# Unit maxima by way of memory in place of a product of ones

## The chip, the cores and the metric

The kernel runs on one core of a Trainium2 chip. The metric is device time in microseconds (us) of one execution. A core has TensorE (PE, matmuls; PEld are its weight loads), VectorE (DVE), ScalarE (ACT), GpSimd (POOL) and SyncE (SP), which here only issues transfers. Each engine works through its own queue in order. Times are given as a median of several executions; one further execution is taken with the hardware profiler, and its trace gives all rows that are shown here.

## The reference: what is computed

There are 8 batches of 8 heads, 576 positions and 64 channels per head. An attention without a score matrix comes first, then two layers that mix over positions and over channels:

```python
q_s = softmax(q, axis=-1)                    # over the 64 channels
k_s = softmax(k, axis=2)                     # over the 576 positions
kv  = einsum('bhsd,bhse->bhde', k_s, v)
x   = einsum('bhsd,bhde->bhse', q_s, kv)     # heads side by side: x is (8, 576, 512)
xt  = x.transpose(0, 2, 1)
u   = x + (relu(xt @ w_tok1) @ w_tok2).transpose(0, 2, 1)     # 576 -> 256 -> 576
out = u + relu(u @ w_ch1) @ w_ch2                             # 512 -> 1536 -> 512
```

Both softmaxes subtract the maximum first. The one that matters here is k's: one maximum for each of the channels, taken over all positions.

## The kernel before

The attention and the first mixing layer work on *units*: two heads of one batch, 128 channels side by side. There are 8 x 4 = 32 units, numbered from 0; NJ is 4, the units of a batch. The second mixing layer works on 9 groups of 512 rows of u; for each group it runs 12 *steps* (f). A step is `ch1` (line 409: 12 matmuls of 128 x 512 into a bank of the PSUM ring `ps_h`), an eviction by ACT (line 412, `h2h`) and by DVE (line 413, `h2l`, the rest that the first rounding leaves), and `ch2` (line 421: 12 matmuls into the four `ps_o` banks). The `ch2` of a step stands behind the `ch1` of the next.

A unit goes through these stages: its loads (`load_unit`: `kt` with the channels on partitions, line 137; `q`, line 140; `k` with the positions on partitions, line 144), `softmax_k` and `softmax_q`, then `stage_qT` (transposes q), `stage_kv` (line 277: 20 records of small matmuls, k's exponentials against v with a column of ones for the sums), `stage_y` (line 337), `stage_h1` (line 345) and two halves of `stage_u` (line 381). The first NE = 8 units are done ahead of the steps ("early"); the other 24 are dealt out between the steps by the table `todo`: at its own step a unit n runs `stage_qT` and `stage_kv`, then `softmax` of unit n + 1, then, half a step later, the loads of unit n + 2.

In a late unit `k` lies with positions on partitions, while the maximum is found from `kt` by DVE as one value for each of 128 partitions (`mc`, line 219). To subtract it, the maximum of every channel must stand in every partition. That is done in lines 233 to 236: ACT writes a diagonal matrix `dg` with the maxima, PE multiplies a matrix of ones by it into a bank of `ps_h`, and ACT copies the result to `mb`. POOL then subtracts `mb` from `k` (line 237) and ACT takes the exponential (line 238). `mb` and `dg` have one buffer each, `mc` two, `k` and `q` two, `kt` and `v` one.

What sets the order: the kernel's text gives a priority by its order, and the builder lays out each engine's queue with a model of durations, so that an engine may run ahead of the text where its buffers allow. All loads are on SP's queue (`v`, lines 154 and 155, is issued in `stage_kv`, for the next unit). The results go out on ACT's queue (line 454). `split` (lines 114 and 115) makes a rounded copy on ACT and the rest on DVE or, for `qh` and `ql`, on POOL.

Of the kernel before, what the change touches and what calls it, by code (L numbers as in the profile page):

```python
# [8 lines left out]
F32 = mybir.dt.float32  # L9
F32R = mybir.dt.float32r  # L10
U32 = mybir.dt.uint32
AF = mybir.ActivationFunctionType
# [3 lines left out]
P = 128  # L16
# [4 lines left out]
def attn_mixer_kernel(ctx: ExitStack, tc: tile.TileContext, q, k, kt, v, wt, out, dims):  # L21
# [3 lines left out]
    nc = tc.nc  # L25
    B, H, S, D, TOK, DM, DCH, wide = dims
    NJ = DM // P
# [8 lines left out]
    NE = 2 * NJ  # L36
# [13 lines left out]
    ident = const.tile([P, P], F32R, name="ident")  # L50
# [11 lines left out]
    ones = const.tile([P, P], F32, name="ones")  # L62
# [26 lines left out]
    dg = lay.tile([P, P], F32, name="dg")  # L89
    for i in range(3):  # L90
        slots[i][1] = lay.tile([P, NJ, CW], F32R, name=f"ul{i}")
    mb = lay.tile([P, P], F32, name="mb")
# [16 lines left out]
    def f32(ap):  # L109
        return ap.bitcast(F32)  # L110
# [8 lines left out]
    def ps_unit(dtype=F32):  # L119

        pools = unit_banks[0]
        pool, name = pools[turn[0] % len(pools)]
        turn[0] += 1
        return pool.tile([P, 512], dtype, name=name)
# [88 lines left out]

    turned_k = []

    def softmax_k(u):
        ktt = u["kt"]
        mc = sm.tile([P, 1], F32, name="mc")
        nc.vector.tensor_reduce(mc, ktt, axis=AX.X, op=ALU.max)  # L219
        kx = u["k"]  # L220
        if u["early"]:
            nc.vector.tensor_scalar(mc, mc, -1.0, None, op0=ALU.mult)
            nc.scalar.activation(ktt, ktt, AF.Exp, bias=mc)
            t = ps_unit()
            for c in range(C):
                nc.tensor.transpose(t[:, c * P : (c + 1) * P], ktt[:, c * P : (c + 1) * P], f32(ident))
            nc.scalar.copy(kx[:, 0:C, :], t.rearrange("p (c d) -> p c d", c=C))
            t = ps_unit()
            turned_k.append(nc.tensor.transpose(t[:, 0:P], ktt[:, S0 : S0 + P], f32(ident)).ins)
            nc.scalar.copy(kx[:, C, :], t[:, 0:P])  # L230
            return

        nc.scalar.activation(dg, f32(ident), AF.Copy, scale=mc)
        t = ps_unit()
        nc.tensor.matmul(t[:, 0:P], ones, dg, start=True, stop=True)  # L235
        nc.scalar.copy(mb, t[:, 0:P])  # L236
        nc.gpsimd.tensor_tensor(kx, kx, mb.unsqueeze(1).broadcast_to([P, C1, P]), op=ALU.subtract)  # L237
        nc.scalar.activation(kx, kx, AF.Exp)

# [223 lines left out]
    def soft(n):  # L463
        if n < NU:
            softmax_k(units[n])
            softmax_q(units[n])
# [194 lines left out]
```

## Time and profile before

| | us |
|---|---|
| median of 3 executions (lowest to highest) | 822.23 (821.69 to 822.65) |
| the profiled execution | 822.09 |
| its span, first to last instruction | 820.3 |
| PE busy | 803.5 (98%) |
| PE weight loads busy | 678.1 (83%) |
| DVE busy | 490.5 (60%) |
| ACT busy | 340.0 (41%) |
| POOL busy | 84.4 (10%) |

The time of the profiled execution and its span differ by 1.8 us, which lie outside the first and the last instruction. A row of a group gives line, engine, operation, the tiles written and read with their shapes, the count, then busy time in us and the mean duration in ns, and last the idle time of the engine just before these instructions with what ended it. A row of the order of time gives start, duration, engine, line and operation; neighbours of one kind are merged ("x20"), with in brackets an idle time before them. A row of the chain of waits gives start and length of a piece of the chain that ended last. SPq is SP's queue: an issue of a transfer. Matmuls overlap each other in the trace; a matmul's start is recorded, its end is modelled.

### The profile page before, as it was taken

The numbers are of one execution on the slowest core, as the hardware profiler recorded it, in microseconds if no ns is written. First come the engines' busy times: TensorE is split into PE (matmuls) and PEld (weight loads), VectorE is DVE, ScalarE is ACT, GpSimd is POOL, SyncE is SP. The second block draws the span as 40 slices with busy tenths as digits, with TensorE's granted clock in tenths as the row PEclk, the third lists the DMA queues.
The fourth block names the chain that finished last, engine by engine and source line by source line (L and its number), as shares of the span: only waits on it lengthen the run. The fifth ranks groups of instructions, "written<-read, shape, count | busy, mean of one in ns | idle before, by whom it ended". The sixth has DMA issues, their size and how long they took to land.

```text
span 820.3 us, 11946 instructions
## 1 busy us (share of the span) xinstructions
PE 803.5 (98%) x4512; PEld 678.1 (83%) x4512; DVE 490.5 (60%) x1104; ACT 340.0 (41%) x898; POOL 84.4 (10%) x69
## 2 busy tenths in 40 slices
PE   7899999989999999999999999999999999999997
PEld 6688888878888888888888888888888888888886
DVE  6999998897875455855576555845575324113112
ACT  6976564457544344443434443434443421101110
POOL 1000010102201011111111111101111100000100
PEclk9999999999999999999999999999999999999999
DMA  9753433424222112312232221312121001001001
GB/s 298 241 161 93 150 108 113 139 83 126 64 73 85 48 53 63 109 52 64 64 114 63 64 64 35 113 47 63 39 91 48 15 1 51 1 1 51 1 1 51
DMA packets 60634, 63.55 MB, mean 77 GB/s; under 512 B 40865, under 2 KB 40993, under 8 KB 60577
## 3 DMA queue, kind: packets, MB, share of 16 engines
q1 hardware_dynamic: 55392, 53.36, 22.2%
q10 hardware_dynamic: 5184, 9.44, 3.1%
q8 instruction: 35, 0.57, 0.3%
q14 instruction: 23, 0.18, 0.1%
HBM read 53.35 MB, written 9.44 MB: 77 GB/s over the span
## 4 chain that ended last, share of the span: by engine, by line
PE 89%; DVE 6%; DMA 3%; ACT 1%; SPq 1%; issue 0%; DVEq 0%; ACTq 0%
PE ps_h L409 34%; PE ps_o L421 34%; PE ps_h L381 8%; PE ps_h L337 5%; PE ps_h L277 2%; DMA stg<-in_w 2%; PE ps_h L345 1%; DMA kt_t<-in_kt 1%; PE ps_o L381 1%; PE ps_h L235 1%; PE ps_o L337 1%; DVE mc L219 1%; DVE q_t L323 1%; DVE cv_s L176 1%; DVE cv_s L181 1%; DVE stg L179 0%
## 5 line engine op out<-in xcount | busy, mean ns | idle before, releaser
L409 PE MATMUL ps_h<-uh,cw 128*128 128x512 f32 x864 | 268.6, 391 | 0.3 <-DVE cw L115 0.3
L421 PE MATMUL ps_o<-h2h,cw 128*128 128x512 f32 x864 | 250.0, 392 | 2.2 <-DVE cw L115 2.2
L421 PEld LDWEIGHTS ps_o<-h2h,cw 128*128 128x128 f32 x864 | 160.0, 188 | 34.7 <-ACT h2h L412 2.4
L409 PEld LDWEIGHTS ps_h<-uh,cw 128*128 128x128 f32 x864 | 159.3, 188 | 31.6 <-DVE cw L115 0.8
L413 DVE SCALAR_TENSOR_TENSOR h2l<-ps_h,h2h 128x512 fp32r<-128x512 f32 x108 | 74.3, 688 | 170.4 <-ACT h2h L412 170.2
L412 ACT ACTIVATE h2h<-ps_h 128x512 fp32r<-128x512 f32 x108 | 64.4, 596 | 253.8 <-PE ps_h L409 251.5
L409 PE MATMUL ps_h<-ul,cw 128*128 128x512 f32 x432 | 168.7, 390 | 0.0
L421 PE MATMUL ps_o<-h2l,cw 128*128 128x512 f32 x432 | 151.9, 394 | 0.0
L409 PEld LDWEIGHTS ps_h<-ul,cw 128*128 128x128 f32 x432 | 81.1, 188 | 17.4
L421 PEld LDWEIGHTS ps_o<-h2l,cw 128*128 128x128 f32 x432 | 79.7, 188 | 15.9
L323 DVE COPY q_t<-cv_s 32x160 f32<-32x160 f32 (+1 forms) x264 | 62.1, 235 | 45.2 <-POOL ql L115 41.9
L237 POOL TENSOR_TENSOR k_t<-k_t,mb 128x640 f32<-128x640 f32 x24 | 38.0, 1583 | 350.6 <-ACT mb L236 350.6
L115 POOL TENSOR_TENSOR ql<-q_t,qh 128x640 fp32r<-128x640 f32 x24 | 39.2, 1633 | 220.7 <-ACT qh L114 218.2
L245 DVE TENSOR_REDUCE st<-q_t 128x10 f32<-128x640 f32 x32 | 26.2, 817 | 38.2 <-DMA q_t<-in_q 38.2
L323 ACT COPY q_t<-cv_s 32x128 f32<-32x128 f32 (+1 forms) x120 | 36.8, 307 | 2.1 <-DVE cv_s L315 0.7
L256 ACT ACTIVATE q_t<-q_t 128x640 f32<-128x640 f32 x24 | 17.7, 739 | 40.4 <-DVE q_t L255 40.4
L381 PE MATMUL ps_h<-w2h,hh 128*128 128x256 f32 (+1 forms) x112 | 32.6, 299 | 0.0
L381 PE MATMUL ps_h<-w2l,hh 128*128 128x256 f32 (+1 forms) x112 | 32.6, 296 | 0.0
L389 DVE TENSOR_TENSOR ul<-ps_h,uh 128x320 fp32r<-128x320 f32 (+4 forms) x76 | 26.8, 372 | 7.4 <-ACT uh L388 6.8
L388 ACT CAST uh<-ps_h 128x320 fp32r<-128x320 f32 (+4 forms) x76 | 24.4, 337 | 15.6 <-PE ps_h L381 11.2
L381 PE MATMUL ps_h<-w2h,hl 128*128 128x320 f32 (+1 forms) x112 | 29.8, 300 | 0.3 <-DVE hl L353 0.2
L219 DVE TENSOR_REDUCE mc<-kt_t 128x1 f32<-128x640 f32 x32 | 25.9, 809 | 4.8 <-DMA kt_t<-in_kt 3.5
(144 smaller groups left out, 1077.8 us busy)
## 6 DMA issues: line engine op xcount, KB each, us to landing
stg<-in_w SPq DMA_DIRECT2D x28, 512.0 KB, 4.0
kt_t<-in_kt SPq DMA_DIRECT2D x32, 320.0 KB, 3.2
q_t<-in_q SPq DMA_DIRECT2D x32, 320.0 KB, 3.1
v_t<-in_v SPq DMA_DIRECT2D x64, 128.0 KB, 2.6
out<-stg ACTq DMA_DIRECT2D x32, 256.0 KB, 2.1
k_t<-in_k SPq DMA_DIRECT2D x24, 320.0 KB, 3.3
v_t<-in_v SPq DMA_DIRECT2D x32, 32.0 KB, 2.5
out<-part ACTq DMA_DIRECT2D x4, 256.0 KB, 2.3
```

The source lines that it names most:

```text
L115: lo_eng.tensor_tensor(lo, src, f32(hi), op=ALU.subtract)
L219: nc.vector.tensor_reduce(mc, ktt, axis=AX.X, op=ALU.max)
L237: nc.gpsimd.tensor_tensor(kx, kx, mb.unsqueeze(1).broadcast_to([P, C1, P]), op=ALU.subtract)
L245: nc.vector.tensor_reduce(st[:, 0, :], qt, axis=AX.X, op=ALU.max)
L323: eng(qx[ys, 0:n, xs], turned[xs, 0:n, ys])
L337: nc.tensor.matmul(y[:, 0:TOK], a, w, start=(i == 0), stop=(i == len(mm) - 1))
L381: nc.tensor.matmul(t[:, 0:N], a, w, start=(i == 0), stop=(i == len(mm) - 1))
L389: nc.vector.tensor_tensor(ul, src, f32(uh), op=ALU.subtract).ins,
L409: nc.tensor.matmul(t, cw[f][x][:, n, :], w, start=(i == 0), stop=(i == 3 * NJ - 1))
L412: nc.scalar.activation(hh, t, AF.Relu).ins,
L413: nc.vector.scalar_tensor_tensor(hl, t, 0.0, f32(hh), op0=ALU.max, op1=ALU.subtract).ins,
L421: nc.tensor.matmul(o, cw[f][x][:, n, :], w, start=(first and i == 0), stop=(last and i == 2))
```

## The change

From unit NE + NJ = 12 on, the maximum takes another way to all partitions: `mc` is written to a row of 128 values in memory, and that row is read back into `mb`, the same row for each of the 128 partitions. Both transfers are on SP's queue; the second reads what the first has written. The row has two buffers. `dg`, the product of ones and the copy to `mb` remain for units 8 to 11; units 0 to 7 never had them.

```diff
+    THROUGH = NE + NJ
+    dram = ctx.enter_context(tc.tile_pool(name="dram", bufs=2, space=bass.MemoryType.DRAM))
...
-        nc.scalar.activation(dg, f32(ident), AF.Copy, scale=mc)
-        t = ps_unit()
-        nc.tensor.matmul(t[:, 0:P], ones, dg, start=True, stop=True)
-        nc.scalar.copy(mb, t[:, 0:P])
+        if u["n"] < THROUGH:
+            nc.scalar.activation(dg, f32(ident), AF.Copy, scale=mc)
+            t = ps_unit()
+            nc.tensor.matmul(t[:, 0:P], ones, dg, start=True, stop=True)
+            nc.scalar.copy(mb, t[:, 0:P])
+        else:
+            row = dram.tile([1, P], F32, name="row")
+            nc.sync.dma_start(row.rearrange("o p -> p o"), mc)
+            nc.sync.dma_start(mb, row.broadcast_to([P, P]))
         nc.gpsimd.tensor_tensor(kx, kx, mb.unsqueeze(1).broadcast_to([P, C1, P]), op=ALU.subtract)
         nc.scalar.activation(kx, kx, AF.Exp)
```

## The prediction

> **What bounds the kernel now.** I read the profile page's busy times first, then the same by stage, then the groups of the changed lines, then the order of instructions around one unit. The busy times, and the stages (columns: stretch, length, busy time and count of PE, PEld, DVE, ACT, POOL, granted clock, DMA share, GB/s):
>
> ```profile
> span 820.3 us, 11946 instructions
> PE 803.5 (98%) x4512; PEld 678.1 (83%) x4512; DVE 490.5 (60%) x1104; ACT 340.0 (41%) x898; POOL 84.4 (10%) x69
> ...
> 150.00:200.00 50.00, 46.92 (x285) 39.17 (x284) 41.49 (x97) 29.29 (x96) 6.27 (x4) 1.00 0.35 103
> 200.00:242.00 42.00, 42.00 (x253) 35.93 (x252) 32.74 (x75) 21.53 (x53) 7.65 (x5) 1.00 0.25 69
> ...
> 260.00:650.00 390.00, 390.00 (x2282) 329.89 (x2281) 231.50 (x538) 161.51 (x393) 55.23 (x36) 1.00 0.23 66
> 650.00:820.00 170.00, 165.13 (x770) 137.30 (x768) 38.17 (x71) 23.03 (x47) 6.34 (x5) 1.00 0.05 19
> ```
>
> From 200 us to 650 us, where the changed units lie, TensorE has no idle time at full clock; ACT and DVE are busy 41% and 59% of 260 to 650 us (161.51 and 231.50 of 390) and POOL 14%. So the end is set by how much work stands in PE's queue, and what another engine saves is worth nothing by itself. Work taken out of PE's queue moves everything behind it forward one for one, as long as PE never begins to wait.
>
> The groups of the product of ones and its neighbours, from the lists of their lines:
>
> ```profile
> L235 PE MATMUL ps_h<-dg,ones 128*128 128x128 f32 x48 | 11.4, 319 | 0.4 <-DVE h2l L413 0.4
> ...
> L235 PE MATMUL ps_h<-dg,ones x48: 270/275/377, 146.1 to 642.3; 128*128 128x128 f32 x48
> L233 ACT ACTIVATE dg<-ident,mc x24: 402/404/412, 96.0 to 620.6; 128x128 f32<-128x128 f32 x24
> L236 ACT COPY mb<-ps_h x24: 245/248/267, 147.0 to 642.6; 128x128 f32<-128x128 f32 x24
> L237 POOL TENSOR_TENSOR k_t<-k_t,mb x24: 1564/1570/1862, 147.4 to 643.0; 128x640 f32<-128x640 f32 x24
> L219 DVE TENSOR_REDUCE mc<-kt_t x32: 762/810/821, 3.7 to 576.9; 128x1 f32<-128x640 f32 x32
> ```
>
> A product of ones is two matmul records: 48 for the 24 late units. Its maximum is ready long before: the last mc starts at 576.9 us, its product at 642.2, its subtraction at 643.0. The product waits not for data but for its turn in PE's queue.
>
> **The change part by part.** NE is 8 and NJ is 4, so units 12 to 31 change: 20 of the 24 late units.
>
> *Removed from PE: 20 products.* Their busy time overlaps that of the neighbours, so I price them from start to start. Two units with the product, and the last unit, behind whose kv there is none:
>
> ```profile
> 239.04 0.80 PE L277 MATMUL ps_h<-v_t,k_t 128*64 128x65 f32 x20
> 239.78 0.49 PE L235 MATMUL ps_h<-dg,ones 128*128 128x128 f32 x2
> 240.02 0.71 PE L421 MATMUL ps_o<-h2h,cw 128*128 128x512 f32 x2
> ...
> 641.38 0.80 PE L277 MATMUL ps_h<-v_t,k_t 128*64 128x65 f32 x20
> 642.12 0.49 PE L235 MATMUL ps_h<-dg,ones 128*128 128x128 f32 x2
> 642.36 0.71 PE L421 MATMUL ps_o<-h2l,cw 128*128 128x512 f32 x2
> ...
> 663.50 0.80 PE L277 MATMUL ps_h<-v_t,k_t 128*64 128x65 f32 x20
> 664.24 0.72 PE L421 MATMUL ps_o<-h2l,cw 128*128 128x512 f32 x2
> ```
>
> From the start of kv to the next kind of work it is 0.74 us in all three (239.78 - 239.04, 642.12 - 641.38, 664.24 - 663.50), whether a product follows or not. The product itself then holds the queue for 0.24 us (240.02 - 239.78, 642.36 - 642.12), 0.12 per record. So 20 x 0.24 = 4.8 us leave the bound engine. Its weight loads go with it; they run beside matmuls.
>
> The Trainium skill, "TensorE: Matmul & The Clock Gate", section "Back-to-back issue gap", gives about 81 ns per matmul of 128 columns in a stream of weight loads and matmuls. By that an estimate for 40 records is 40 x 0.081 = 3.2 us and the sum below would be 818.9 instead of 817.3; this trace's 0.12 us per record decides.
>
> *Removed from ACT:* 20 x (0.404 + 0.248) = 13.0 us of copies. ACT has 228 us idle of the 390, so I value this at nothing. A PSUM bank of the ps_h ring is no longer taken for the product; PE does not wait there, so nothing again.
>
> *Added: two transfers per unit on SP's queue.* One writes 128 single values to memory, the other reads that row into all partitions (64 KB). No such transfer is in the trace. The nearest landings, and the queue around one unit:
>
> ```profile
> v_t<-in_v SPq DMA_DIRECT2D x64, 128.0 KB, 2.6
> out<-stg ACTq DMA_DIRECT2D x32, 256.0 KB, 2.1
> k_t<-in_k SPq DMA_DIRECT2D x24, 320.0 KB, 3.3
> v_t<-in_v SPq DMA_DIRECT2D x32, 32.0 KB, 2.5
> ...
> 552.78 0.93 SPq L154 DMA_DIRECT2D v_t<-in_v  x2
> 553.81 0.60 SPq L155 DMA_DIRECT2D v_t<-in_v  x1
> 554.46 0.59 SPq L144 DMA_DIRECT2D k_t<-in_k  x1
> 555.80 0.34 SPq L137 DMA_DIRECT2D kt_t<-in_kt  x1
> 570.77 0.33 SPq L140 DMA_DIRECT2D q_t<-in_q  x1
> ...
> SPq L140 <- DVE qtl L115: 274.4, 20, 15.7
> ```
>
> For the write the lower bound is the output's 2.1 us (also a write to memory), for the read v's 2.5; the upper bound for both is twice the 3.3 of k, as single values are much smaller pieces than any here. I take 2.5 and 2.6, by the two v rows, which are nearest in size: 5.1 us from issue to broadcast maximum, bounds 4.6 and 13.2. The wait of the second for the first holds SP's queue for about 2.5 us (2.1 to 6.6); queued behind it are kt, q, k and v of later units. Between the kt issue (555.80) and the next q (570.77) SP waits 15 us for VectorE to free q's buffer, the 15.7 of the last row. Both transfers fit there, their wait at the upper bound too. If that cover were gone, v, which has one buffer and loads between two kv products (the starts at 552.78 for its issue and, in the chain row under A, 574.27 for its next reader), would be the first to be late: it has 21.5 us less 1.6 of issuing and 2.5 of landing, 17 us to spare.
>
> *Moved: the subtraction, its exponential and the order around them.* The subtraction's wait for mb ends today with PE's turn. Afterwards it ends with the transfers or, as mb can come a unit ahead, with k's own load: issued at 554.46, landed 3.3 us later, so about 557.8, some 18.6 us ahead of its place today (576.36 in the rows below). The exponential follows. Neighbours in their queues:
>
> ```profile
> 557.90 0.60 ACT L412 ACTIVATE h2h<-ps_h 128x512 fp32r<-128x512 f32 x1 [1.14 <-PE ps_h L409]
> 559.58 0.73 ACT L114 CAST qh<-q_t 128x640 fp32r<-128x640 f32 x1 [1.08 <-PE ps_h L337]
> ...
> 560.43 1.57 POOL L115 TENSOR_TENSOR ql<-q_t,qh 128x640 fp32r<-128x640 f32 x1 [4.45 <-ACT qh L114]
> 576.36 1.57 POOL L237 TENSOR_TENSOR k_t<-k_t,mb 128x640 f32<-128x640 f32 x1 [14.35 <-ACT mb L236]
> ...
> 569.25 0.69 DVE L413 SCALAR_TENSOR_TENSOR h2l<-ps_h,h2h 128x512 fp32r<-128x512 f32 x1 [2.89 <-ACT h2h L412]
> ...
> 570.61 2.75 PE ps_h L409 x12
> 573.36 0.91 PE ps_o L421 x4
> ```
>
> A subtraction of 1.57 us from 557.8 ends at 559.4, ahead of ql at 560.43; should it come late it delays ql by 1.57 us at most. The exponential can delay qh by one instruction, under a microsecond. What PE needs next from these engines has room: h2l is done at 569.94 and PE begins to read it at 573.36, 3.4 us later. So I cost the move at nothing.
>
> *The sum.* The profiled execution took 822.09 us, its span is 820.3. 822.09 - 4.8 = 817.3. The median of the three is 822.23, 0.14 above the profiled one, so against it 817.4.
>
> **The rivals.**
>
> *A: the product was worth more.* The chain of waits, which goes from end to end, gives each product 0.42 us:
>
> ```profile
> 574.27 0.73 PE ps_h L277 x20
> 575.00 0.42 PE ps_h L235 x2
> ```
>
> At 0.42 x 20 = 8.4 us it would be 813.7 on the profile's time, 813.8 against the median. Against it: part of that is the latency of one product, under which the next matmul already starts, as the start-to-start rows show.
>
> *B: the gain is given back.* A changed order of instructions, laid out by the builder's own model of durations, opens gaps in PE of about 5 us in all: 822. For it: the stage from 150 to 200 us has 3.1 us of PE idle (50 - 46.92), so gaps do occur where the weight transfers run. Against it: the changed units begin behind that stage.
>
> *C: slower, ACT is held at the exponential.* ACT's queue is in order, and the eviction h2h stands in it beside the exponential, which waits for POOL, which now waits for a transfer. If the build's order puts the exponential where its model has the transfers landed, and they land later, h2h and h2l behind it are late; from a hold of 3.4 us on (the room above) PE waits. Break-even is a hold of 3.4 + 0.24 = 3.64 us in each unit. A hold of 4.0 us would cost 20 x 0.6 = 12 us less the 4.8: 829. For it: the chain of two transfers, 5.1 us, is longer than the room, and its write of single values is the least known price here. Against it: the maximum is there a whole unit or more ahead, so the transfers can be issued long before the exponential's turn, and today's holds at this instruction sum to 11.1 us in 15 times, none over 1.7:
>
> ```profile
> ACT k_t L238 <- POOL k_t L237: 11.1, 15, 1.7
> ```
>
> The Trainium skill speaks against the change here: "DMA: Bandwidth & Descriptors", section "Two DMAs through the same engine are not ordered", has the issuing engine wait for the first transfer's semaphore before it issues one that reads the same bytes, and the section "Anatomy of one DMA — SWDGE (gpsimd) path" puts the fixed cost of one, mostly the receipt from memory, at about 2 us. By that an estimate of the pair is 4 us, spent in the queue for half of it. The write of the output, 2.1 us for 256 KB, agrees with a fixed cost of that size; no row here shows a transfer that waits for another's landing.
>
> *D: it does not do what it says* (fewer products leave, or none): 822. All 20 units pass the branch that the diff changes, so little speaks for it.
>
> **How the numbers follow.** The forecast 0.77, with its own range from 816.4 to 818.6 (a product between 0.18 and 0.29 us: the lower end allows for part of it having filled a gap that kv leaves, the upper for a little relief elsewhere); A 0.05; B 0.08; C 0.08; D 0.02. What a measurement of this kernel can tell from no change is about 0.2%, 1.6 us: faster means under 820.6, slower above 823.9. Faster is the forecast and A, 0.82; the same is B and D, 0.10; slower is C, 0.08. The range from 816.0 to 821.0 leaves out A, C, D and most of B, and holds a gain half eaten by new gaps. The unknown landings enter the sum only through C, whose time lies outside.
>
> **What would show it.** In the profile of the changed kernel the group of the product should have 8 records in place of 48; between the start of kv and the next ps_o or ps_h matmul there should be 0.74 us in units 12 to 31; PE from 200 to 650 us should still have no idle time, and what lies behind 650 us should be the same work about 4.8 us earlier. POOL's subtraction should wait for a transfer (mb or k), not for ACT, and stand some 15 to 19 us earlier in the unit. The transfers should land in 2 to 3.3 us each, and SP's wait for the first inside its idle time. I am wrong if PE shows waits on h2h or h2l in this stretch (C), if idle time of PE appears around 200 us or the order of kv has moved (B), or if the distance behind kv shrinks by more than 0.24 us (A).

## The result and the profile after

The changed kernel takes **964.06 us** (median of 6, 960.73 to 967.72) against 822.0 us before (median of 6, 820.60 to 823.94): 1.173 times as long, 95% interval 1.170 to 1.176. The forecast was 817.4 us with a range from 816.0 to 821.0, so even the sign was wrong. The profiled execution took 963.29 us; its span is 961.5.

First the page of the changed kernel: busy times, then PE's busy tenths and its granted clock in 40 slices of 24 us each, then the shares of the chain of waits by line.

```profile
PE 834.4 (87%) x4472; PEld 696.9 (72%) x4472; DVE 497.2 (52%) x1104; ACT 331.1 (34%) x858; POOL 86.3 (9%) x69
...
PE   7899999455656363699999999999999999999997
...
PEclk8999999757777676899999999999999999999999
...
PE ps_h L418 26%; PE ps_o L430 26%; DMA kt_t<-in_kt 21%; PE ps_h L390 6%; PE ps_h L346 4%; DVE mc L223 2%; PE ps_h L286 2%; DMA q_t<-in_q 1%; DMA stg<-in_w 1%; PE ps_h L354 1%; PE ps_o L390 1%; DVE cv_s L176 1%; SPq L244 1%; PE ps_o L346 0%; ACT q_t L260 0%
```

PE has lost 40 instructions, as forecast (4512 to 4472), but it is no longer busy throughout: in the slices from the eighth to the seventeenth, some 168 to 409 us, it is about half idle and its granted clock falls. The chain now runs through the load of `kt` for 21% of the span, about 202 us; before, that was 1%.

The same by stage, after and then before (columns as in the prediction):

```profile
163.00:400.00 237.00, 126.16 (x538) 101.70 (x538) 86.10 (x191) 50.06 (x147) 15.83 (x10) 0.74 0.61 54
400.00:805.00 405.00, 405.00 (x2339) 341.55 (x2339) 231.73 (x544) 158.32 (x372) 56.81 (x35) 0.99 0.21 55
805.00:961.50 156.50, 151.30 (x698) 125.63 (x692) 32.33 (x54) 18.10 (x34) 5.03 (x4) 1.00 0.06 21
```

```profile
163.00:256.00 93.00, 89.92 (x533) 76.48 (x532) 71.89 (x174) 49.41 (x150) 14.12 (x9) 1.00 0.28 85
256.00:664.00 408.00, 408.00 (x2390) 345.35 (x2390) 239.70 (x560) 168.53 (x410) 56.54 (x36) 1.00 0.22 63
664.00:820.30 156.30, 151.13 (x692) 125.47 (x686) 32.14 (x54) 18.08 (x34) 5.03 (x4) 1.00 0.06 21
```

The whole loss lies in one stretch. What PE did in 93 us (533 instructions) takes 237 us (538), 144 us more. Idle time of PE grows by 107.8 us (237 - 126.16 less 93 - 89.92), and the same matmuls are busy 36.2 us longer (126.16 - 89.92), at a granted clock of 0.74 in place of 1.00. From 400 to 805 us PE has no idle time again, and the tail is the same work in nearly the same time. The Trainium skill, "TensorE: Matmul & The Clock Gate", Part 1, says that PE's clock gate lets through half the clock after an idle window of some 3.4 us, and nothing between half and all. The trace agrees: behind a wait of 4.62 us that ends at 353.47 us, matmuls of 128 x 512 start 0.43 us apart from 354.06 to 356.62 us and 0.23 us apart from 357.16 us on. So the 0.74 is read as a mixture of both.

Between the first kv record of unit 18 and the last of unit 31 there are 13 products in the kernel before and none after. The kv records of these 14 units, before and then after (last two times: first and last start):

```profile
L277 PE MATMUL ps_h<-v_t,k_t x280: 220/222/272, 373.4 to 664.1; 128*64 128x65 f32 x140
```

```profile
L286 PE MATMUL ps_h<-v_t,k_t x280: 220/222/272, 517.3 to 805.3; 128*64 128x65 f32 x140
```

290.7 us have become 288.0: a product was worth 2.7 / 13 = 0.21 us to the bound engine, where the forecast had 0.24.

Two transfers are slow (median landing in the last column):

```profile
kt_t<-in_kt SPq DMA_DIRECT2D x32, 320.0 KB, 10.3
...
row<-mc SPq DMA_DIRECT2D x20, 0.5 KB, 8.3
```

The write of 512 bytes takes 8.3 us, over three times what was forecast, and `kt`, 3.2 us before, takes 10.3 when it is issued right behind one. A write and the next unit's `kt` alternate on SP's queue in turns of 12 us. There follow one such turn in the chain of waits, then the groups of both transfers' issues with their first and last start, then a wait of SP's queue (us in total, times, longest):

```profile
352.84 0.33 SPq L244
353.26 10.76 DMA kt_t<-in_kt
364.11 0.83 DVE mc L223
364.96 0.33 SPq L244
```

```profile
L244 SPq DMA_DIRECT2D row<-mc x20: 319/326/343, 163.4 to 399.1; - x20
...
L245 SPq DMA_DIRECT2D mb<-row x20: 320/339/342, 256.0 to 747.4; - x20
```

```profile
SPq L244 <- DVE mc L223: 121.9, 12, 12.3
```

All 20 writes are issued between 163.4 and 399.1 us, which is exactly the bad stretch; the reads of `mb` reach to 747.4 us. The writes have run up to 350 us ahead of need. The turn kt, `mc`, write, kt takes 12 us, and SP, in order, stands at the write until the next `mc` is there: 121.9 us in 12 waits. The `q`, `k` and `v` of the units on which PE is working stand behind it.

What PE itself waits for is the other end of that turn, DVE. DVE's queue is in order too: it stands at the maximum until `kt` has landed, and the results that PE needs stand behind the maximum. There follow the same turn on DVE and PE, the waits between 160 and 400 us, and the same wait of DVE in the whole kernel before:

```profile
352.00 0.82 DVE L223 TENSOR_REDUCE mc<-kt_t 128x1 f32<-128x640 f32 x1 [9.21 <-DMA kt_t<-in_kt]
352.73 0.68 DVE L422 SCALAR_TENSOR_TENSOR h2l<-ps_h,h2h 128x512 fp32r<-128x512 f32 x1
...
353.47 0.79 PE L430 MATMUL ps_o<-h2l,cw 128*128 128x512 f32 x1 [4.62 <-DVE h2l L422]
```

```profile
DVE mc L223 <- DMA kt_t<-in_kt: 140.9, 18, 10.4
...
PE ps_h L390 <- DVE hl L362: 40.7, 5, 15.5
...
PE ps_o L430 <- DVE h2l L422: 22.9, 5, 5.0
```

```profile
DVE mc L219 <- DMA kt_t<-in_kt: 3.5, 4, 1.8
```

DVE is busy for 86.1 of the 237 us, and 140.9 of the other 150.9 are this one wait. PE's waits in the stretch sum to 110.8 us, 104.8 of them for results of DVE and none for a transfer. So `kt`, slowed behind the write, holds DVE, and DVE holds PE; the loads of `q`, `k` and `v` stand behind the write as well, but PE is not seen to wait for them.

Before, the `mc` buffer of a unit came free when ACT had made `dg` of it, and `dg` when PE had taken the product, one unit's turn at a time. Now the write itself frees it, so nothing is left that ties the maxima to the pace of the units. The row sets no limit either: the pool is asked for two buffers, but the built program gives each of the 20 units a row of its own, and in the trace all 20 writes are out when only four reads are.

### The profile page after: what moved, and what is told of

It is laid out like the page before. It is cut to its first block, busy times and chain, and to the rows that moved or that the text cites. A ratio compares the mean times of both kernels' runs of the same rounds, so it can differ in the third digit from the quotient of the medians.

```text
span 961.5 us, 11916 instructions
## 1 busy us (share of the span) xinstructions
PE 834.4 (87%) x4472; PEld 696.9 (72%) x4472; DVE 497.2 (52%) x1104; ACT 331.1 (34%) x858; POOL 86.3 (9%) x69
## 4 chain that ended last, share of the span: by engine, by line
PE 68%; DMA 24%; DVE 5%; ACT 1%; SPq 1%; issue 1%; DVEq 0%; ACTq 0%
PE ps_h L418 26%; PE ps_o L430 26%; DMA kt_t<-in_kt 21%; PE ps_h L390 6%; PE ps_h L346 4%; DVE mc L223 2%; PE ps_h L286 2%; DMA q_t<-in_q 1%; DMA stg<-in_w 1%; PE ps_h L354 1%; PE ps_o L390 1%; DVE cv_s L176 1%; SPq L244 1%; PE ps_o L346 0%; ACT q_t L260 0%
## 5 line engine op out<-in xcount | busy, mean ns | idle before, releaser
L418 PE MATMUL ps_h<-uh,cw 128*128 128x512 f32 x864 | 278.2, 403 | 16.4 <-ACT mb L241 6.0
L430 PE MATMUL ps_o<-h2h,cw 128*128 128x512 f32 x864 | 257.4, 402 | 29.1 <-DVE part L461 14.6
L430 PEld LDWEIGHTS ps_o<-h2h,cw 128*128 128x128 f32 x864 | 164.9, 194 | 64.8 <-issue 13.3
L418 PEld LDWEIGHTS ps_h<-uh,cw 128*128 128x128 f32 x864 | 165.5, 196 | 51.1 <-ACT mb L241 6.7
L430 PE MATMUL ps_o<-h2l,cw 128*128 128x512 f32 x432 | 158.2, 412 | 22.9 <-DVE h2l L422 22.9
L418 PE MATMUL ps_h<-ul,cw 128*128 128x512 f32 x432 | 172.5, 399 | 0.0
L430 PEld LDWEIGHTS ps_o<-h2l,cw 128*128 128x128 f32 x432 | 82.8, 196 | 42.3 <-DVE h2l L422 25.0
L223 DVE TENSOR_REDUCE mc<-kt_t 128x1 f32<-128x640 f32 x32 | 26.1, 816 | 143.8 <-DMA kt_t<-in_kt 143.8
L418 PEld LDWEIGHTS ps_h<-ul,cw 128*128 128x128 f32 x432 | 83.9, 194 | 18.7
L246 POOL TENSOR_TENSOR k_t<-k_t,mb 128x640 f32<-128x640 f32 x24 | 39.8, 1660 | 534.1 <-DMA k_t<-in_k 233.6
L390 PE MATMUL ps_h<-w2h,hl 128*128 128x320 f32 (+1 forms) x112 | 33.7, 331 | 40.7 <-DVE hl L362 40.7
L390 PEld LDWEIGHTS ps_h<-w2h,hl 128*128 128x128 f32 x112 | 22.5, 212 | 41.8 <-DVE hl L362 41.8
## 6 DMA issues: line engine op xcount, KB each, us to landing
kt_t<-in_kt SPq DMA_DIRECT2D x32, 320.0 KB, 10.3
```

The costliest lines, as they stand in the source:

```text
L390: nc.tensor.matmul(t[:, 0:N], a, w, start=(i == 0), stop=(i == len(mm) - 1))
L418: nc.tensor.matmul(t, cw[f][x][:, n, :], w, start=(i == 0), stop=(i == 3 * NJ - 1))
L430: nc.tensor.matmul(o, cw[f][x][:, n, :], w, start=(first and i == 0), stop=(last and i == 2))
```

## The experiments

The expectations give each theory a name. In every one the question is what the slow row write does: stand in the wrong place on SP's queue, hold whatever waits for it, slow the other transfers, or matter less than the changed order of the work.

### The write alone, with the product kept

The kernel before, with one write of the row more in units 12 to 31. Nothing reads the row; the maximum still goes through the product.

```diff
...
+        if u["n"] >= NE + NJ:
+            row = dram.tile([1, P], F32, name="row")
+            nc.sync.dma_start(row.rearrange("o p -> p o"), mc)
```

> The kernel before, with the write of the 128 maxima to memory added for units 12 to 31; nothing reads the row, the product of ones stays. Here the buffer of mc is freed by ACT's dg as before, so the units stay paced by PE, and the write stands behind k's load in SP's queue. Theory 'queue' (the loss comes from writes of later units that stand ahead of the loads of the current ones, and each turn kt, mc, write, kt takes 12 us): 822 within 2 us, with the write landing in about 8 us and a kt behind it in about 10, both inside SP's idle time. Rival 'write' (the small pieces load the transfer engines, about 7 us lost per unit whatever the order): 940 or more. Rival 'order' (running ahead alone is enough, the size of the pieces does not matter): 822.

Measured: 825.41 us against 822.18, ratio 1.0042 (1.0027 to 1.0056): 3.2 us more, where at most 2 were expected, and far from the 940 of rival 'write'. Its transfers and its stretch of 250 to 650 us:

```profile
kt_t<-in_kt SPq DMA_DIRECT2D x32, 320.0 KB, 8.1
...
row<-mc SPq DMA_DIRECT2D x20, 0.5 KB, 7.5
...
250.00:650.00 400.00, 400.00 (x2335) 338.60 (x2334) 235.77 (x554) 165.59 (x404) 55.34 (x36) 1.00 0.37 66
```

The write is as slow here, and `kt` behind it too, yet PE has no idle time: the product still paces the units, and nobody waits for the row. So slow transfers alone don't make the 142 us. They may make the 3 us by which the median is above; the execution that was profiled (822.06 us) was the fastest of them, so its trace does not show where these lie.

### The size of the write

The same added write with 128, 64, 32 or 16 of the values, by the unit's number. The row is not read and only partly written.

```diff
...
+            m = (128, 64, 32, 16)[u["n"] % 4]
+            nc.sync.dma_start(row.rearrange("o p -> p o")[0:m], mc[0:m])
```

> As the kernel before with the unused write added, but the write has 128, 64, 32 and 16 values in turn (unit number modulo 4). Time about 822. If every single value costs about 1 us on its transfer engine (128 values are 8 on each of 16 engines) the landings are about 8, 5, 3 and 2 to 2.5 us; if the 8 us is a fixed cost of a write to memory from many partitions, all are near 8.

One execution: 824.37 us. The landings, in the order 128, 64, 32, 16 values (sizes are rounded in the view):

```profile
row<-mc SPq DMA_DIRECT2D x5, 0.5 KB, 8.0
row<-mc SPq DMA_DIRECT2D x5, 0.2 KB, 7.4
row<-mc SPq DMA_DIRECT2D x5, 0.1 KB, 4.4
row<-mc SPq DMA_DIRECT2D x5, 0.1 KB, 2.4
```

16 values land like any small transfer, 128 need over three times as long. In these four rows bytes and pieces shrink together; that the pieces cost and not the bytes shows beside the 32 KB of `v`, which landed in 2.5 us before, and below, where the same 512 bytes go out in four pieces. The packets of the whole execution, before and with 20 writes of 128 values:

```profile
DMA packets 60634, 63.55 MB, mean 77 GB/s; under 512 B 40865, under 2 KB 40993, under 8 KB 60577
```

```profile
DMA packets 63513, 63.56 MB, mean 77 GB/s; under 512 B 43744, under 2 KB 43872, under 8 KB 63456
```

(63513 - 60634) / 20 = 144 packets more per write: 128 for its single values and 16 more, for with the four sizes, 60 values in the mean, it is (62153 - 60634) / 20 = 76. The Trainium skill, "DMA: Bandwidth & Descriptors", section "Rules for kernel authors", has a strided last dimension lowered to one descriptor per element; the packets agree. What that costs in time stands in the four rows.

### Both transfers behind the same unit's k

If only the place on SP's queue were wrong, tying both transfers behind the load of `k` of their own unit should give the gain back.

```diff
-            nc.sync.dma_start(t.rearrange("p c d -> p (c d)"), k[n])
+            u["k_load"] = nc.sync.dma_start(t.rearrange("p c d -> p (c d)"), k[n]).ins
...
+            with tc.issue_after(u["k_load"]):
+                nc.sync.dma_start(row.rearrange("o p -> p o"), mc)
+                nc.sync.dma_start(mb, row.broadcast_to([P, P]))
...
```

> The changed kernel, with both transfers of a unit put behind the load of the same unit's k in SP's queue; nothing else is changed, the write keeps its 128 single values. Theory 'queue': the loss is gone, 817 to 819, PE without idle time from 200 us on, SP held 8 us by the wait for the write inside its idle time of 15 us. Rival 'write': about 960. Rival 'order': 817 to 819.

Measured: 957.1 us, ratio 1.163 (1.160 to 1.166): hardly better. The theory that only the place on SP's queue matters has fallen. The number is the one of rival 'write', but the added write that nobody reads excludes that rival. And it is another loss: spread over all changed units, with PE at 288 of 337 us in the first half and 258 of 302 in the second.

```profile
163.00:500.00 337.00, 287.68 (x1535) 238.87 (x1533) 170.78 (x405) 115.20 (x297) 36.90 (x24) 0.92 0.26 61
500.00:802.00 302.00, 257.81 (x1349) 212.03 (x1349) 133.46 (x330) 92.06 (x222) 32.17 (x21) 0.90 0.22 48
```

Its waits (us in total, times, longest), and one unit in order of time:

```profile
POOL k_t L247 <- DMA mb<-row: 497.0, 20, 32.2
...
ACT k_t L248 <- POOL k_t L247: 186.5, 22, 12.6
...
PE ps_h L391 <- ACT hh L362: 55.7, 15, 6.6
```

```profile
290.96 0.42 SPq L245 DMA_DIRECT2D row<-mc  x1
...
298.69 0.33 SPq L246 DMA_DIRECT2D mb<-row  x1
...
303.00 1.56 POOL L247 TENSOR_TENSOR k_t<-k_t,mb 128x640 f32<-128x640 f32 x1 [25.39 <-DMA mb<-row]
304.52 1.56 POOL L115 TENSOR_TENSOR ql<-q_t,qh 128x640 fp32r<-128x640 f32 x1
304.60 0.74 ACT L248 ACTIVATE k_t<-k_t 128x640 f32<-128x640 f32 x1 [8.40 <-POOL k_t L247]
```

The write at 290.96 keeps `mb` from being issued until 298.69; POOL subtracts at 303.00; `ql`, behind it in POOL's queue, and ACT's exponential wait for that, ACT with 8.4 us of idle time, and `hh` behind the exponential is what PE waits for. This is rival C of the prediction, with its place as named and a hold of 8.5 us in the mean (186.5 / 22) and 12.6 at most in place of 4. It suggests a **late write**: the builder laid out the queues for a write that lands fast, and whichever in-order queue waits for it holds what stands behind.

### Four pieces in place of 128 values

DVE transposes blocks of 32 x 32, so that the maxima lie as four pieces of 32 values, which are written as pieces of 128 bytes; the maxima and the pieces stand in columns of `dg`, which these units no longer use; the order is left to the builder.

```diff
...
+            nc.vector.transpose(flat, col)
-            nc.sync.dma_start(row.rearrange("o p -> p o"), mc)
+            nc.sync.dma_start(row.rearrange("o (a c) -> (o a) c", a=P // Q), flat.rearrange("(a b) c -> a b c", b=Q)[:, 0, :])
```

> The changed kernel, with the maxima turned by DVE into four rows of 32 first, so that the write has 4 pieces of 128 bytes in place of 128 of 4 bytes; nothing holds back the order, the writes may run ahead as in the changed kernel. Theory 'queue' with the slow turn: the write lands in 2 to 3 us, kt behind it in 3 to 4, a turn takes about 5 us in place of 12, so most of the 142 us is gone: 817 to 850. Rival 'write': 817 to 822. Rival 'order': 930 or more, nearly as slow as the changed kernel.

Measured: 827.92 us, ratio 1.0079 (1.0054 to 1.0104). One pair of issues, the group of the writes, and the stretch from 150 to 200 us:

```profile
204.89 0.61 SPq L248 DMA_DIRECT2D row<-dg  x1
206.69 0.33 SPq L249 DMA_DIRECT2D mb<-row  x1
```

```profile
L248 SPq DMA_DIRECT2D row<-dg x20: 477/494/612, 204.9 to 287.5; - x20
```

```profile
150.00:200.00 50.00, 43.81 (x256) 36.62 (x254) 39.23 (x94) 29.32 (x95) 6.70 (x4) 1.00 0.28 86
```

Now the read can be issued 1.8 us after the write, where the unit above needed 7.7, and of 142 us only 6 are left. The writes still run far ahead of their reads, all 20 of them in 83 us, but about 4 us apart in place of 12, and DVE's waits for `kt` sum to 16.2 us in place of 143.8 in the whole execution. The length of the write is thus the cause of all but a few per cent of the loss, with the unpaced order as its way: the same order costs little when the write is short. What is left lies between 150 and 300 us: PE is idle there for 11.1 us, 6.2 of them before 200 us, where before it was 3.1 in all.

### Four pieces, behind the same unit's k

The two edits above together.

> Both edits together: the write in 4 pieces of 128 bytes, and both transfers behind the load of the same unit's k. The first series spoke against 'queue' as it stood: with the transfers behind k the time stayed at 957, because POOL's subtraction, laid out for a fast write, waited 11 us longer for mb and held ql, the exponential and the evictions behind it. New theory 'late write' (the queues are laid out for a write of some 2 us; the write of single values takes 8, and whichever in-order queue waits for it holds what stands behind): with a fast write nothing is held, 817 to 820, PE without idle time from 200 us on, that is 4.8 us below the kernel before. Rival 'place' (transfers behind k are bad whatever they take, since SP, POOL and DVE wait for them): 880 or more. Rival 'no gain' (the products left PE but something else costs the same): 822.

Measured: 824.71 us, ratio 1.0019 (1.0007 to 1.0031): the gain that was expected is not there.

```profile
150.00:200.00 50.00, 44.18 (x256) 36.95 (x254) 39.54 (x94) 29.63 (x95) 6.69 (x4) 1.00 0.29 87
200.00:250.00 50.00, 47.72 (x287) 40.09 (x287) 38.33 (x88) 21.11 (x51) 8.29 (x5) 1.00 0.36 95
```

5.8 + 2.3 us of idle time between 150 and 250 us, 5.0 more than before, eat the 4 us that the missing products save later. At the start of that stretch the last weights are converted (the last one starts at 169.7 us). Two explanations stand here: the reuse of `dg` for the pieces, just where its last products run, or the stretch itself, which does not bear the new order.

### The slow write with a unit's lead

Single values again, but issued behind `k` of the unit before, with two buffers for `mb` (the second is `dg`) and four for `mc`.

```diff
...
-        mc = sm.tile([P, 1], F32, name="mc")
+        mc = sm.tile([P, 1], F32, name="mc", bufs=4)
+        mb = mbs[u["n"] >= THROUGH and u["n"] % 2]
...
+            with tc.issue_after(units[u["n"] - 1]["k_load"]):
+                nc.sync.dma_start(row.rearrange("o p -> p o"), mc)
+                nc.sync.dma_start(mb, row.broadcast_to([P, P]))
```

> The slow write of 128 single values again, but issued one unit earlier: behind the load of the k of the unit before, with two buffers for the broadcast maximum (dg, which these units do not use, is the second) and four for mc, so that neither the subtraction nor the next maximum has to wait for it. Theory 'late write': the 8 us are covered by a unit of 22 us, 817 to 822 (up to 3 us of it for loads slowed by the pieces, as the unused write alone measured 825.4 against 822.2). Rival 'traffic' (the slow pieces themselves cost the time by slowing other transfers): 850 or more.

Measured: 845.35 us, ratio 1.0276 (1.0254 to 1.0299). A lead of a unit takes away five sixths of the loss (142 to 22 us), not all of it. The number lies between the theory and the rival that has the other transfers slowed. The waits show a hold that neither foresaw:

```profile
DVE mc L224 <- DMA row<-mc: 66.7, 15, 7.4
```

DVE can't write the next `mc` before a row write has let go of its buffer: the ring of four only lets the maxima run further ahead until it is full, and then DVE, in order, stands up to 7.4 us with PE's evictions behind it.

### The transfers on ACT's queue

```diff
-            nc.sync.dma_start(row.rearrange("o p -> p o"), mc)
-            nc.sync.dma_start(mb, row.broadcast_to([P, P]))
+            nc.scalar.dma_start(row.rearrange("o p -> p o"), mc)
+            nc.scalar.dma_start(mb, row.broadcast_to([P, P]))
```

> The changed kernel, with both transfers issued from ACT's queue instead of SP's, nothing else changed. Theory 'late write': ACT's queue then waits for the write, 8 us a unit, with evictions behind it that have 3.4 us to spare, so PE waits about 4 us or more a unit: 880 to 1000. Rival 'SP' (the loss comes only from SP's loads held back): 817 to 830.

One execution: 907.35 us. SP's loads now stand behind no write, and 84 us are still lost, again in an early stretch:

```profile
200.00:300.00 100.00, 67.80 (x333) 54.80 (x331) 42.96 (x101) 28.45 (x82) 9.91 (x6) 0.83 0.56 77
```

The rival that blames only SP's loads has fallen. PE now waits for ACT as well (between 200 and 400 us 11.7 us for `h2h` and 9.3 us for `hh`), but DVE still stands at the maximum for `kt` too, 61.3 us in 12 waits. So this is not ACT's queue alone.

### Four pieces that never touch dg

The pieces are turned inside `kt`'s own buffer, which is free once the maximum is found; both transfers behind the same unit's `k`.

```diff
...
+            nc.vector.tensor_copy(ktt[:, 0:1], mc)
+            nc.vector.transpose(ktt[:, Q : 2 * Q], ktt[:, 0:Q])
+            with tc.issue_after(u["k_load"]):
+                nc.sync.dma_start(row.rearrange("o (a c) -> (o a) c", a=P // Q), ktt[:, Q : 2 * Q].rearrange("(a b) c -> a b c", b=Q)[:, 0, :])
+                nc.sync.dma_start(mb, row.broadcast_to([P, P]))
```

> As the kernel with four pieces behind k, but the maxima are turned inside kt's own buffer, whose contents are no longer needed, instead of in dg, so that unit 12's maximum need not wait for the last product of ones. In that kernel the starts of kv show 0.21 us gained in each unit from the fourteenth on, and 6.4 us lost between units 8 and 13, where the conversions of the last weights end. Theory 'start' (the loss lies in the order of this stretch alone, and dg's reuse makes it): 818 to 820.5, kv of unit 13 at most 2 us later than before. Rival 'stretch' (any changed unit that falls into the stretch of the weights loses there, whatever holds its maxima): 822 to 826, with the loss again between units 8 and 13.

Measured: 825.27 us, ratio 1.0033 (1.0020 to 1.0045). The reuse of `dg` is not the reason: the loss is there without it.

### The same pieces, a unit earlier

Behind `k` of the unit before, two buffers for `mb`.

> The same four pieces in kt's buffer, issued one unit earlier, behind the load of the k of the unit before, with dg as the second buffer of the broadcast maximum. Theory 'late write': more room for the transfers changes nothing where PE has no idle time, so within 1 us of the kernel that issues them behind the same unit's k; the wait of the subtraction for mb should be gone. Rival 'stretch': 822 to 826.

Measured: 821.44 us, ratio 0.9988 (0.9978 to 0.9997): 3.8 us better than behind the same unit's `k`, where at most 1 was expected, and hardly to be told from no change. So lead, or the second buffer for `mb` that came with it, counts even for a fast write; these runs do not separate the two.

### From the seventeenth unit on

The pieces in `kt`, behind the same unit's `k`, but for units 16 to 31 only, so that the conversion of the weights is over.

```diff
-    THROUGH = NE + NJ
+    THROUGH = NE + 2 * NJ
```

> Four pieces in kt's buffer behind the same unit's k, but only from unit 16 on, behind the stretch of the weights: 16 products leave PE. Theory 'start' and rival 'stretch' both: 16 x 0.21 = 3.4 us gained, 818 to 820, 3.4 below the kernel before. Rival 'first units' (the first changed units lose some 6 us wherever they stand, because the queues change over there): 823 to 826.

Measured: 820.90 us against 822.50, ratio 0.9981 (0.9972 to 0.9990): the best version of this study, a gain of 1.6 us (0.19%), about half of the 3.4 that were expected and hardly to be told from no change.

```profile
150.00:200.00 50.00, 47.77 (x291) 40.26 (x290) 42.59 (x100) 29.93 (x99) 6.34 (x5) 1.00 0.36 106
200.00:250.00 50.00, 50.00 (x293) 42.77 (x292) 38.23 (x88) 24.29 (x60) 9.67 (x6) 1.00 0.29 86
```

Without the four units that fall into the early stretch, PE is busy there as before or better. The last kv record starts at 660.6 us, 3.5 us ahead of the 664.1 before, about the 16 x 0.21 = 3.4 us of the sum. But 0.9 of it is there ahead of unit 16 already, so part is the changed order and not the products, and the profiled execution was the fastest of the eleven (818.64 us beside a median of 820.90). The medians bear out 1.6 us and not 3.5.

### The slow write with a lead, from the seventeenth unit on

> The slow write of 128 single values issued one unit early, with the second broadcast buffer and four of mc, but only from unit 16 on. The same kernel from unit 12 on measured 845, with 22 us lost between units 10 and 13 and only 0.02 us gained per unit behind them, where 0.21 were to be had. Theory 'late write': behind the weights' stretch an early issue covers the 8 us, 819 to 823. Rival 'traffic': the slow pieces cost time wherever they stand, 830 or more.

Measured: 834.18 us against 822.37, ratio 1.0136 (1.0109 to 1.0163). With the early stretch taken out, the slow write still loses 12 us though it has a lead. 'Late write' has failed here as it stood (819 to 823), and the number is one of rival 'traffic' (830 or more).

```profile
DVE mc L224 <- DMA row<-mc: 46.3, 11, 5.9
```

PE is idle for 28.0 us in all (832.0 - 804.04), 11.2 more than before, and its waits for DVE follow the hold of DVE at the ring of `mc`: DVE begins a maximum at 414.69 us after 5.92 us of waiting, `h2l` stands behind it, and PE goes on at 416.16 us after 1.32 us of waiting for that `h2l`; the same happens at 483.99 and 485.46 us. How much slowed transfers add to that these runs don't separate. In the first experiment, where nobody waits for the row, 20 writes went with some 3 us.

### The change for the last ten units only

The changed kernel with the two transfers as they are, for units 22 to 31.

```diff
-    THROUGH = NE + NJ
+    THROUGH = 22
```

> The changed kernel, unchanged in its order and its write of single values, but only for units 22 to 31. Theory 'late write' with SP's queue as the place: the writes run ahead again as soon as they may, near unit 20 at about 395 us; ten turns of 12 us hold SP for about 120 us, in which PE starves, and the rest runs at full speed: 870 to 910, half of the changed kernel's loss. Rival 'stretch' (the changed kernel lost its time because its first units fall among the weights): 815 to 835.

One execution: 896.3 us. Half the units, half the loss (74 of 142 us), in a stretch that begins 213 us later:

```profile
400.00:500.00 100.00, 49.18 (x205) 39.84 (x206) 25.05 (x57) 13.12 (x32) 4.66 (x3) 0.71 0.53 42
```

The ten writes are issued from 376.5 to 484.4 us, one after the other as in the full change, and PE stands for half of that time; DVE waits there 82.3 us in 9 waits for `kt` at the maximum. So it is the turns of the unpaced writes, about 7 us lost for each, and not what else happens at 165 us.

## Why the prediction was wrong, point by point

- **PE is the bound and a product is worth 0.24 us: right.** 0.21 us was measured per product once the queues flow (4.2 us for 20), and rival A's 0.42 is out.
- **The write's landing, 2.5 us with bounds 2.1 and 6.6: the term that was mis-sized.** It takes 8.3 us, above its upper bound, and the pair 8.3 + 2.8 = 11.1 us in place of 5.1. Both ends came from rows of large pieces; the sentence that made single values the reason for the upper bound had the right concern, but doubling a load's time was no bound. With 1.8 us to the next issue in its place nearly all of the loss is gone, as the four pieces showed.
- **"Both transfers fit there" (SP's 15 us of idle time): the step that failed.** That idle time was read from the order of the queue before. The change takes away `dg` and the product, and these were what paced the maxima; the writes of all 20 units moved ahead of the loads, in turns of 12 us, and SP stood at them for 121.9 us. I counted each removed instruction's time but not the wait that it had imposed on others.
- **"v ... would be the first to be late", and the landings enter "only through C": wrong.** What came late was `kt`, whose load right behind a write took 10.3 us in place of 3.2. It held DVE at the maximum for 140.9 us, and PE waited 104.8 us for results of DVE. The sum had no term for a load slowed by the write ahead of it, nor for DVE's queue.
- **"The maximum is there a whole unit or more ahead", used against C:** true, and the harm came from it: what may run ahead does, to the cost of what stands behind it.
- **Rival C:** its kind was right, an in-order queue held by a late transfer, its queue was not: SP's and DVE's in the changed kernel; ACT's with the transfers behind `k`, where its hold was 8.5 us in the mean, and in part with the transfers on ACT's own queue. A chance of 0.08 was too low for the one price that no row showed.
- **Rival B's mechanism** (new gaps around 200 us that eat the gain) is what the versions with a fast write from unit 12 on met: 5.0 to 11.1 us of idle time of PE between 150 and 300 us, where 3.1 were before. "The changed units begin behind that stage" was wrong: their loads and maxima run ahead into it.
- **The signs:** POOL's subtraction does wait for a transfer (233.6 us for `k`), the product's records are down by 40, and the tail is as long as before. "2 to 3.3 us each" fails at the write, and with it SP's wait within its idle time; PE without idle time from 200 us on fails up to 400 us.

## What to carry to other kernels

Ask of every removed instruction which wait it imposed: where it freed a buffer at the pace of the bound engine, its removal lets a producer run ahead, on a queue that others need. Running ahead cost some 6 us with a short write and 142 with a long one. Ask also which in-order engine will stand at the slowed transfer, and what of the bound engine's needs is queued behind it. A transfer of single 4-byte values is priced by its pieces, not by its bytes; turn the values into rows first (here 32 x 32 blocks on DVE). And idle time of a queue is cover only as long as the order that left it idle still holds.

## What the runs showed of the hardware that was not expected

- A write of 128 single values from 128 partitions to memory lands in 7.5 to 8.3 us (medians of three kernels); 64, 32 and 16 values in 7.4, 4.4 and 2.4 us, so it is not in proportion.
- A load of 320 KB issued right behind such a write lands in 8.1 to 10.3 us instead of 3.2 (medians of the added write and of the changed kernel), and in 4.1 where the read of the row stands between. In the bad stretch the DMA engines are busy 0.61 of the time and move 54 GB/s, where before 0.28 sufficed for 85 GB/s.
- A quarter of the loss, 36 of 144 us, is not idle time of PE but longer busy time at a lower clock: 0.74 granted over 237 us. An estimate from the clock alone is 89.92 / 0.74 - 89.92 = 31.6 us.
- Left open: where the 3 us of the added, unread write lie, how much the slowed transfers cost beside the waits they cause, and what opens PE's gaps between 150 and 300 us where the write is fast.
